# Two of six pairs of weight blocks in chunks 2 to 5 computed as seven half-size products

## The chip, the cores and the metric

One core of a Trainium2 chip. The metric is the device time of one execution in microseconds (us), as a median over executions. Most executions of a kernel agree within 0.3%; now and then one is some per cent longer, and those are left out. Profile times ("span") run from the first to the last instruction and are some 2 us shorter than the measured time. TensorE multiplies matrices, VectorE, ScalarE and GpSimd work elementwise; in profile lines they are PE, DVE, ACT and POOL, and PEld is TensorE's loading of weights.

## The reference, cut to what matters

Attention with keys and values averaged over 8 positions, then a gated feed-forward layer:

```python
q, k, v: (8 batches, 8 heads, 576, 64)
k_p, v_p = mean of 8 neighbours of k, v              # 72 keys per head
x = softmax(q @ k_p.T / 8) @ v_p                     # -> 4608 tokens x 512
h = relu(x @ w_gate) * (x @ w_val)                   # 512 -> 1536, twice
out = h @ w_out                                      # 1536 -> 512
```

## The kernel before

The 4608 tokens pass in nine chunks (0 to 8) of 512. While TensorE computes the hidden layer of chunk c, it also takes the output product of chunk c-1 and the attention of the next batch. Values are f16, sums in PSUM f32. Below, a unit is a block of the hidden layer or an output product in the order of the chunk's program; pieces of attention stand between units.

A block of the hidden layer is 128 of its 1536 columns. In chunks 0 to 5 each of twelve blocks is computed plainly:

```python
def gate_val(c, fo, t0=0, n=TCH):
    ...
    for w in (wg_sb, wv_sb):
        t = ps_mm.tile([P, TCH], F32, ...)           # one PSUM bank
        ... nc.tensor.matmul(out=t[...], lhsT=w[:, ci, fsl], rhs=x_T[...])   # 4 of 512 columns
        ps.append(t)
    nc.scalar.activation(out=relu[:, :n], in_=ps[0][:, :n], func=AF.Relu)
    nc.vector.tensor_tensor(out=h_tiles[c][:, fo, ...], in0=ps[1][:, :n], in1=relu[:, :n], op=ALU.mult)
```

The output product of every chunk already uses a scheme of the Strassen-Winograd kind: split both matrices in four, form sums of quarters, and seven half-size products do the work of eight. It needs four sums of h (`S`, two instructions each, VectorE) and four of the weights (`T`, once):

```python
sums = [... add(k, x, y, op, half)
        for k, x, y, op in ((0, d1, d, ALU.add), (1, S[0], a, ALU.subtract),
                            (2, a, d1, ALU.subtract), (3, b, S[1], ALU.subtract))
        for half in range(2)]
...
SUMS_AT = [1, 2, 3, 4, 5, 6, 13, 14]     # after which unit of the chunk each of the eight stands
```

In chunks 7 and 8, and at the end of 6, the hidden layer uses such a scheme too. Between these units stand the pieces of attention values. A piece fills two PSUM banks, and VectorE empties each with a reciprocal and a multiplication; the next piece waits for a free bank of three:

```python
def values(b, t):
    for half in range(2):
        ps = ps_at.tile([P, 512], F32, name="at_ps", tag="at_ps")     # bufs=3
        ... matmuls into ps ...
        nc.vector.reciprocal(out=rd[:n, half], in_=pv[:, :, D:D + 2])
        nc.vector.tensor_tensor(out=x[...], in0=..., in1=rd[...], op=ALU.mult)
```

GpSimd averages k and v in "trees" of additions and issues their loads.

The softmax here doesn't subtract the row's maximum and nothing guards it: scores larger than these inputs give would overflow.

## Time and profile before

| | before |
|---|---|
| time, median of 3 | 328.61 us (328.54 to 330.12) |
| span | 327.4 us, full clock |
| TensorE, VectorE, GpSimd busy | 97%, 69%, 63% |
| chain of waits: TensorE, VectorE | 89%, 6% |
| length of chunks 2, 3, 4, 5 | 34.98, 33.79, 34.00, 34.21 us |

A chunk's length is read from the timeline of TensorE, from the start of its k transposes to those of the next chunk. The lines behind the other rows, and how they are read, are in the prediction.

### The profile page before, as it was taken

How to read it: one execution, taken by the hardware profiler on the slowest of the kernel's cores; microseconds unless marked ns; L12 is line 12 of the kernel's file. 1: busy time of each engine (PE TensorE's matmuls, PEld its weight loads, DVE VectorE, ACT ScalarE, POOL GpSimd, SP SyncE). 2: the span in 40 equal slices, each digit the busy share in tenths (PEclk: the TensorE clock that was granted, in tenths of full speed). 3: DMA queues.
4: the chain of work that ended last, by engine and by line, in shares of the span. 5: the costliest groups of instructions: out<-in, count | busy, mean ns of one | idle time of the engine just before them, and what ended most of it. 6: DMA issues, size and time to landing. Idle time of an engine off the chain costs nothing.

```text
span 327.4 us, 7013 instructions
## 1 busy us (share of the span) xinstructions
PE 318.7 (97%) x2670; PEld 226.9 (69%) x2670; DVE 226.2 (69%) x482; ACT 151.2 (46%) x353; POOL 206.9 (63%) x258
## 2 busy tenths in 40 slices
PE   8899999999999999999999999999999999999995
PEld 3577885455566656665898867655667888888674
DVE  7465737677684864696387745784779989879762
ACT  1454482364466226612672257225825565565330
POOL 8556607999999942965199309999901577667300
PEclk9999999999999999999999999999999999999999
DMA  7999998996958538999794472223012130130035
GB/s 110 186 203 202 200 211 151 200 173 118 187 101 159 100 91 86 78 154 160 159 169 76 87 104 60 33 47 124 3 24 50 34 96 2 22 111 2 10 112 137
DMA packets 51010, 35.46 MB, mean 108 GB/s; under 512 B 30432, under 2 KB 45024, under 8 KB 50976
## 3 DMA queue, kind: packets, MB, share of 16 engines
q0 software_dynamic: 18304, 18.88, 36.5%
q1 hardware_dynamic: 32528, 16.00, 26.2%
q8 instruction: 21, 0.34, 0.4%
q10 hardware_dynamic: 144, 0.13, 0.1%
q14 instruction: 13, 0.11, 0.1%
HBM read 37.75 MB, written 9.44 MB: 144 GB/s over the span
## 4 chain that ended last, share of the span: by engine, by line
PE 89%; DVE 6%; DMA 2%; issue 1%; POOL 1%; ACT 0%; DVEq 0%; POOLq 0%
PE mm_ps L430 42%; PE acc_ps L523 19%; PE mm_ps L742 9%; PE at_ps L311 4%; PE mm_ps L468 3%; PE at_ps L389 3%; PE mm_ps L602 2%; DMA q<-in_q_dram 2%; PE at_ps L742 2%; DVE px L395 1%; DVE sum L514 1%; DVE h L439 1%; PE mm_ps L412 1%; PE mm_ps L366 1%; DVE px L758 1%
## 5 line engine op out<-in xcount | busy, mean ns | idle before, releaser
L439 DVE TENSOR_TENSOR h<-mm_ps,relu 128x512 f16<-128x512 f32 (+1 forms) x96 | 59.8, 624 | 69.5 <-PE mm_ps L430 59.2
L436 ACT ACTIVATE relu<-mm_ps 128x512 f16<-128x512 f32 (+1 forms) x96 | 52.2, 544 | 100.1 <-PE mm_ps L430 94.6
L430 PE MATMUL mm_ps<-x_T,wv_sb 128*128 128x512 f16 (+1 forms) x432 | 88.4, 332 | 0.4 <-DVE kpT0u L264 0.4
L430 PE MATMUL mm_ps<-x_T,wg_sb 128*128 128x512 f16 (+1 forms) x432 | 88.5, 331 | 0.0
L430 PEld LDWEIGHTS <-wv_sb 128*128 128x128 f16 x432 | 42.1, 98 | 31.2 <-DVE kpT0u L264 0.8
L430 PEld LDWEIGHTS <-wg_sb 128*128 128x128 f16 x432 | 38.9, 97 | 19.7 <-issue 0.3
L325 ACT ACTIVATE expT<-at_ps 72x288 f16<-72x288 f32 (+2 forms) x128 | 38.8, 374 | 14.3 <-PE at_ps L311 14.2
L523 PEld LDWEIGHTS <-sum 128*128 128x128 f16 x336 | 32.0, 98 | 6.3 <-DVE sum L514 0.9
L395 DVE TENSOR_TENSOR px<-at_ps,prd 128x256 f16<-128x256 f32 (+1 forms) x80 | 33.8, 423 | 2.7
L181 POOL TENSOR_TENSOR tree_b<-tree_a 72x256 f32<-72x256 f32 (+1 forms) x42 | 33.5, 797 | 3.3
L764 POOL TENSOR_TENSOR h<-px 128x256 f16<-128x256 f16 x36 | 25.4, 718 | 13.8 <-ACT px L761 12.8
L175 POOL TENSOR_TENSOR tree_a<-k_in 96x512 f32<-96x512 f16 x18 | 21.5, 1196 | 15.2 <-DMA k_in<-in_k_dram 15.2
L523 PE MATMUL acc_ps<-wo_sums,sum 128*128 128x256 f16 x252 | 30.9, 272 | 0.0
L175 POOL TENSOR_TENSOR tree_a<-v_in 72x512 f32<-72x512 f16 x24 | 28.7, 1197 | 0.1
L523 PEld LDWEIGHTS <-h 128*128 128x128 f16 x252 | 23.7, 98 | 2.9
L763 POOL TENSOR_SCALAR px<-px 128x256 f16<-128x256 f16 x12 | 13.0, 1080 | 18.1 <-PE mm_ps L742 15.3
L844 POOL COPY gate<-h 128x1 f16<-128x1 f16 x4 | 1.5, 380 | 33.9 <-DVE h L439 33.9
L523 PE MATMUL acc_ps<-wo_sb,h 128*128 128x256 f16 x168 | 20.6, 272 | 0.0
L514 DVE TENSOR_TENSOR sum<-h 128x768 f16<-128x768 f16 x28 | 19.0, 679 | 0.0
L531 DVE TENSOR_TENSOR rows<-acc_ps,mid 128x512 f32<-128x512 f32 x21 | 14.4, 686 | 4.7 <-PE acc_ps L523 4.6
L389 PEld LDWEIGHTS <-expT 72*128 72x128 f16 (+1 forms) x280 | 12.9, 100 | 5.9 <-DVE prd L394 0.8
L394 DVE RECIPROCAL prd<-at_ps 128x4 f32<-128x4 f32 (+1 forms) x80 | 13.7, 171 | 3.7 <-PE at_ps L389 3.6
(144 smaller groups left out, 527.9 us busy)
## 6 DMA issues: line engine op xcount, KB each, us to landing
out_dram<-rows SPq DMA_DIRECT2D x24, 256.0 KB
k_in<-in_k_dram POOLq DMA_DIRECT2D x7, 576.0 KB, 7.0
q<-in_q_dram POOLq DMA_DIRECT2D x7, 576.0 KB, 10.0
v_in<-in_v_dram POOLq DMA_DIRECT2D x6, 576.0 KB, 12.7
wg_sb<-in_moe_w_gate_dram POOLq DMA_DIRECT2D x6, 256.0 KB, 11.0
wv_sb<-in_moe_w_val_dram POOLq DMA_DIRECT2D x6, 256.0 KB, 10.8
wo_sb<-in_moe_w_out_dram POOLq DMA_DIRECT2D x3, 512.0 KB, 10.7
v_in<-in_v_dram POOLq DMA_DIRECT2D x2, 512.0 KB, 11.9
```

The lines of the kernel that those rows point to most:

```text
L175: eng.tensor_tensor(out=cell["a"][:n], in0=src[:, :, :4 * D], in1=src[:, :, 4 * D:], op=ALU.add)
L181: eng.tensor_tensor(out=cell["c"][:n], in0=a[:n, :, :2 * D], in1=a[:n, :, 2 * D:], op=ALU.add)
L325: nc.scalar.activation(out=out_ap, in_=in_ap, func=AF.Exp, scale=EXP_SCALE)
L389: nc.tensor.matmul(out=ps[:n, c0:c0 + D + 1], lhsT=weights(b, h, t), rhs=stats[b % 2][:SP, g, s0:s0 + D + 1], start=True, stop=True,)
L395: nc.vector.tensor_tensor(out=x[:n, half * NG // 2:(half + 1) * NG // 2, :, :], in0=pv.rearrange("p g (x c) -> p g x c", x=2)[:, :, :, :D] ...
L430: nc.tensor.matmul(out=t[:, lo:hi], lhsT=w[:, ci, fsl], rhs=x_T[:, ci, x0:x0 + hi - lo], start=(ci == 0), stop=(ci == n_co - 1),)
L436: nc.scalar.activation(out=relu[:, :n], in_=ps[0][:, :n], func=AF.Relu)
L439: nc.vector.tensor_tensor(out=h_tiles[c][:, fo, t0:t0 + n], in0=ps[1][:, :n], in1=relu[:, :n], op=ALU.mult)
L514: nc.vector.tensor_tensor(out=S[k][:, i], in0=x[:, i], in1=y[:, i], op=op)
L523: nc.tensor.matmul(out=ps[:, tb, :], lhsT=lhs[:, i, tb * P:(tb + 1) * P], rhs=rhs[:, i, :], start=(first and tb == 0 and i == 0), stop=(tb ...
L742: nc.tensor.matmul(out=ps[key][:, m], lhsT=w_of(m)[:, i], rhs=xs[:, i], start=(first and m == 0 and i == 0), stop=(m == 1 and i == N_CO - ...
L764: nc.gpsimd.tensor_tensor(out=hc[:, fo_out, cols], in0=gv[:, 0], in1=gv[:, 1], op=ALU.mult)
```

## The change

The intent: in chunks 2 to 5, replace plain blocks by seven half-size products for two of the six pairs of blocks (a block and the one 768 columns on), so that TensorE does 28 matmuls of 256 columns in place of 16 of 512 for a pair. The sums of x (VectorE, four per chunk) and of the weights (GpSimd, once, in chunk 1) get buffers of their own. The two pairs (x and y below) stand at the end of the chunk. The fourth h sum moves forward, from after units 13 and 14 to after 10 and 11. Room comes from merged pools, and one weight sum is made in place. Cut to its core:

```diff
+    def pair_products(c, fo):
+        def pr1(): product("a", plain(0, fs), e, ps_mm);       keep("a", "p1")   # ScalarE copies
+        def pr5(): product("c", summed(0), x_sums[c][0], ps_mm); keep("c", "p5")
+        def pr2(): product("b", plain(1, fs), g, ps_at, "at"); take("b", "p1")   # VectorE adds
+        def pr6(): product("a", summed(1), x_sums[c][1]);      keep("a", "u2")
+        def pr3(): product("c", summed(3), h); take("c", "u2"); finish("b", fo, lo)  # relu, GpSimd mult
+        def pr7(): product("a", summed(2), x_sums[c][2]); take("a", "p5"); finish("c", fo, hi)
+        def pr4(): product("a", plain(1, fu), x_sums[c][3]); ... finish("a", n_hf + fo, hi)
+    def pair_units(c, prods, gv):
+        x, y = [pair_products(c, fo) for fo in range(E_PAIRS)]
+        return [lambda: run([x[1], x[5], x[2], x[6], x[3]]), prods[0], x[7],
+                lambda: run([y[1], y[5]]), x[4], lambda: run([y[2], y[6], y[3]]), prods[1], y[7],
+                gv, y[4]]
...
+        EARLY_SUMS_AT = [1, 2, 3, 4, 5, 6, 10, 11]
...
+            elif c < C_HIDDEN - 1:                    # chunks 2 to 5
+                more = x_sums_of(c)
+                run(more[:2])
+                units = [std[0], prods[0], std[1], std[2], prods[1], std[3], prods[2], std[4],
+                         std[5], prods[3], std[6], prods[4]] + pair_units(c, prods[5:], std[7])
...
                 if c == 1:
-                    run(sums[i:i + 1])
+                    run(sums[i:i + 1] if i < 9 else sums[9:] if i == 13 else [])
+                    if i == 11:
+                        early_weight_sums()           # eight on GpSimd
+                elif c < C_HIDDEN - 1:
+                    if i in (7, 9):
+                        more[2 + (7, 9).index(i)]()
+                    if i in EARLY_SUMS_AT:
+                        sums[EARLY_SUMS_AT.index(i)]()
```

(The seven `pr` functions are shown on one line each; `...` marks cuts.)

More of the change, by code (lines that the diff above doesn't have):

```diff
@@ L46 @@
     NI = QT // 2
+    KG_ROWS = POOL // 2
     KP = 12
@@ L58 @@
     vin_pool = ctx.enter_context(tc.tile_pool(name="vin", bufs=2))
-    tree_pool = ctx.enter_context(tc.tile_pool(name="tree", bufs=2))
+    tree_pool = ctx.enter_context(tc.tile_pool(name="tree", bufs=1))
     q16_pool = ctx.enter_context(tc.tile_pool(name="q16", bufs=2))
@@ L66 @@
     half_pool = ctx.enter_context(tc.tile_pool(name="halfp", bufs=1))
-    relu_pool = ctx.enter_context(tc.tile_pool(name="relup", bufs=3))
-    fout_pool = ctx.enter_context(tc.tile_pool(name="foutp", bufs=2))
-    pexp_pool = ctx.enter_context(tc.tile_pool(name="pexpp", bufs=2))
+    relu_pool = ctx.enter_context(tc.tile_pool(name="relup", bufs=5))
+    row_pool = ctx.enter_context(tc.tile_pool(name="rowp", bufs=4))
+    early_pool = ctx.enter_context(tc.tile_pool(name="earlyp", bufs=1))
     piece_pool = ctx.enter_context(tc.tile_pool(name="piecep", bufs=6))
@@ L88 @@
     sel_rest = const_pool.tile([P, SP], F16, name="sel_rest")
-    kg = const_pool.tile([P, QT * 2 // POOL, 2 * D], F16, name="kg")
-    warm_sb = const_pool.tile([P, TCH], F16, name="warm_sb")
+    kg = early_pool.tile([P, 4 * TCH], F16, name="early_x")[:, :QT // KG_ROWS * 2 * D].rearrange(
+        "p (g d) -> p g d", d=2 * D)
+    warm_sb = relu_pool.tile([P, TCH], F16, name="relu")
     stats = [const_pool.tile([P, NG, 4 * D], F16, name=f"stat{i}") for i in range(2)]
@@ L359, in piece_scores @@
         cols = [(j, n * IQ, IQ)] if n < NF else [(0, NF * IQ, RI), (1, NF * IQ, RI)]
-        e = pexp_pool.tile([P, H, P], F16, name="pexp")
+        e = row_pool.tile([P, DM], F32, name="row").bitcast(F16).rearrange("p (h t) -> p h t", h=H)
         for half in range(2):
@@ L472, in part @@
             if hi == n_fo:
-                o = fout_pool.tile([P, DM], F32, name="fout")
+                o = row_pool.tile([P, DM], F32, name="row")
                 if eng is nc.vector:
@@ L486 @@
     HT, HD = TCH // 2, DM // 2
-    wo_sums = const_pool.tile([P, 4, n_hf, HD], F16, name="wo_sums")
+    wo_sums = const_pool.tile([P, 3, n_hf, HD], F16, name="wo_sums")
+    WO_T = [wo_sums[:, 0], wo_sums[:, 1], wo_sb[:, :n_hf, HD:], wo_sums[:, 2]]
     def weight_sums():
@@ L492, in weight_sums @@
         g, h = wo_sb[:, n_hf:, :HD], wo_sb[:, n_hf:, HD:]
-        t1, t2, t3, t4 = [wo_sums[:, i] for i in range(4)]
+        t1, t2, t3, t4 = WO_T
         return [lambda o=o, x=x, y=y, i=slice(i, i + 2): nc.vector.tensor_tensor(
                     out=o[:, i], in0=x[:, i], in1=y[:, i], op=ALU.subtract)
-                for o, x, y in ((t1, f, e), (t2, h, t1), (t3, h, f), (t4, g, t2))
+                for o, x, y in ((t1, f, e), (t2, h, t1), (t4, g, t2), (t3, h, f))
                 for i in range(0, n_hf, 2)]
@@ L504, in out_products @@
         b, d = hc[:, n_hf:, :HT], hc[:, n_hf:, HT:]
-        S = [sum_pool.tile([P, n_hf, HT], F16, name=f"sum{i}") for i in range(4)]
+        S = [sum_pool.tile([P, n_hf, HT], F16, name=f"sum{i}") for i in range(3)]
+        S.append(S[1])
         e, g, h = wo_sb[:, :n_hf, :HD], wo_sb[:, n_hf:, :HD], wo_sb[:, n_hf:, HD:]
-        T = [wo_sums[:, i] for i in range(4)]
+        T = WO_T
         p1, u2, u3 = [mid_pool.tile([P, 2, HD], F32, name=f"mid{i}") for i in range(3)]
@@ L585, in last_products @@
         b, d = hv[:, n_hf:, :, 0], hv[:, n_hf:, :, 1]
-        S = [sum_pool.tile([P, n_hf, HT], F16, name=f"sum{i}").rearrange(
-            "p f (z t) -> p f z t", z=2) for i in range(4)]
+        S = [sum_pool.tile([P, n_hf, HT], F16, name=f"sum{i}") for i in range(3)]
+        S.append(early_pool.tile([P, 2, 3, N_CO, E_COLS], F16, name="early_w").rearrange(
+            "p m s k f -> p (m s k f)")[:, :n_hf * HT].rearrange("p (f t) -> p f t", f=n_hf))
+        S = [t.rearrange("p f (z t) -> p f z t", z=2) for t in S]
         e, g, h = wo_sb[:, :n_hf, :HD], wo_sb[:, n_hf:, :HD], wo_sb[:, n_hf:, HD:]
-        T = [wo_sums[:, i] for i in range(4)]
+        T = WO_T
         A, Bk, C = {}, {}, {}
@@ L673, with early_weight_sums @@
     F_HALF = n_hf * P
+    E_PAIRS = 2
+    E_COLS = E_PAIRS * P
+    early_w = {}
     w_sums, x_sums, mids = {}, {}, {}
+    def early_weight_sums():
+        tl = early_pool.tile([P, 2, 3, N_CO, E_COLS], F16, name="early_w")
+        fs, fu = slice(0, E_COLS), slice(F_HALF, F_HALF + E_COLS)
+        for m, w in enumerate((wg_sb, wv_sb)):
+            s1, s2, s4 = [tl[:, m, i] for i in range(3)]
+            a11, a12 = w[:, :N_CO, fs], w[:, N_CO:, fs]
+            a21, a22 = w[:, :N_CO, fu], w[:, N_CO:, fu]
+            early_w[m] = [s1, s2, a21, s4]
+            for o, x, y, op in ((s1, a21, a22, ALU.add), (s2, s1, a11, ALU.subtract),
+                                (s4, a12, s2, ALU.subtract), (a21, a11, a21, ALU.subtract)):
+                nc.gpsimd.tensor_tensor(out=o, in0=x, in1=y, op=op)
     def hidden_weight_sums():
@@ L686, in hidden_weight_sums @@
         w_sums[0], w_sums[1] = views[:4], views[4:]
-        for f0 in range(0, F_HALF, 2 * P):
+        for f0 in range(E_COLS, F_HALF, 2 * P):
             fs, fu = slice(f0, f0 + 2 * P), slice(F_HALF + f0, F_HALF + f0 + 2 * P)
@@ L697, in x_quarters @@
     def x_quarters(c):
-        x0 = c * TCH % RING
-        return [x_T[:, k * N_CO:(k + 1) * N_CO, x0 + t * HT:x0 + (t + 1) * HT]
-                for k in range(2) for t in range(2)]
+        at = [(c * TCH + t * HT) % RING for t in range(2)]
+        return [x_T[:, k * N_CO:(k + 1) * N_CO, x0:x0 + HT] for k in range(2) for x0 in at]
     def x_sums_of(c):
         e, f, g, h = x_quarters(c)
-        x_sums[c] = [exp_pool.tile([P, 2, HS], F16, name="expT").rearrange(
-            "p x s -> p (x s)")[:, :N_CO * HT].rearrange("p (k t) -> p k t", k=N_CO)
-            for _ in range(4)]
+        if c < C_HIDDEN - 1:
+            tl = early_pool.tile([P, 4 * TCH], F16, name="early_x").rearrange(
+                "p (x k t) -> p x k t", x=4, k=N_CO)
+            x_sums[c] = [tl[:, i] for i in range(4)]
+        else:
+            x_sums[c] = [exp_pool.tile([P, 2, HS], F16, name="expT").rearrange(
+                "p x s -> p (x s)")[:, :N_CO * HT].rearrange("p (k t) -> p k t", k=N_CO)
+                for _ in range(4)]
         t1, t2, t3, t4 = x_sums[c]
@@ L717, in take_mids @@
                      :, :4 * TCH].bitcast(F32).rearrange("p (x t) -> x p t", x=2)]
-        tiles += [fout_pool.tile([P, DM], F32, name="fout") for _ in range(2)]
+        tiles += [row_pool.tile([P, DM], F32, name="row") for _ in range(2)]
         for z in range(2):
@@ L751, in summed @@
         def summed(i):
-            return lambda m: w_sums[m][i][:, :, fs]
+            return lambda m: (early_w if fo < E_PAIRS else w_sums)[m][i][:, :, fs]
         def take(key, mid, fo_out, cols, eng=None):
@@ L808, in hidden_products, with product, plain, summed @@
         return dict(enumerate((pr1, pr2, pr3, pr4, pr5, pr6, pr7, end, later), 1))
+    def pair_products(c, fo):
+        if c not in h_tiles:
+            h_tiles[c] = h_pool.tile([P, n_fo, TCH], F16, name="h")
+        hc = h_tiles[c]
+        fs, fu = slice(fo * P, (fo + 1) * P), slice(F_HALF + fo * P, F_HALF + (fo + 1) * P)
+        e, f, g, h = x_quarters(c)
+        lo, hi = slice(0, HT), slice(HT, TCH)
+        ps, mid, gv = {}, {}, {}
+        def product(key, w_of, xs, pool=None, name="mm"):
+            first = pool is not None
+            if first:
+                ps[key] = pool.tile([P, TCH], F32, name=f"{name}_ps", tag=f"{name}_ps").rearrange(
+                    "p (m t) -> p m t", m=2)
+            for m in range(2):
+                for i in range(N_CO):
+                    nc.tensor.matmul(
+                        out=ps[key][:, m], lhsT=w_of(m)[:, i], rhs=xs[:, i],
+                        start=(first and m == 0 and i == 0), stop=(m == 1 and i == N_CO - 1),
+                        skip_group_check=True,
+                    )
+        def plain(k, cols):
+            return lambda m: (wg_sb, wv_sb)[m][:, k * N_CO:(k + 1) * N_CO, cols]
+        def summed(i):
+            return lambda m: early_w[m][i][:, :, fs]
+        def keep(key, name):
+            mid[name] = row_pool.tile([P, DM], F32, name="row").rearrange("p (m t) -> p m t", m=2)
+            nc.scalar.copy(mid[name], ps[key])
+        def take(key, name):
+            gv[key] = relu_pool.tile([P, TCH], F16, name="relu").rearrange("p (m t) -> p m t", m=2)
+            nc.vector.tensor_tensor(out=gv[key], in0=ps[key], in1=mid[name], op=ALU.add)
+        def finish(key, fo_out, cols):
+            nc.scalar.activation(out=gv[key][:, 0], in_=gv[key][:, 0], func=AF.Relu)
+            nc.gpsimd.tensor_tensor(
+                out=hc[:, fo_out, cols], in0=gv[key][:, 0], in1=gv[key][:, 1], op=ALU.mult)
+        def pr1():
+            product("a", plain(0, fs), e, ps_mm)
+            keep("a", "p1")
+        def pr5():
+            product("c", summed(0), x_sums[c][0], ps_mm)
+            keep("c", "p5")
+        def pr2():
+            product("b", plain(1, fs), g, ps_at, "at")
+            take("b", "p1")
+        def pr6():
+            product("a", summed(1), x_sums[c][1])
+            keep("a", "u2")
+        def pr3():
+            product("c", summed(3), h)
+            take("c", "u2")
+            finish("b", fo, lo)
+        def pr7():
+            product("a", summed(2), x_sums[c][2])
+            take("a", "p5")
+            finish("c", fo, hi)
+        def pr4():
+            product("a", plain(1, fu), x_sums[c][3])
+            relu = relu_pool.tile([P, TCH], F16, name="relu")[:, :HT]
+            nc.scalar.activation(out=relu, in_=ps["a"][:, 0], func=AF.Relu)
+            nc.vector.tensor_tensor(
+                out=hc[:, n_hf + fo, lo], in0=ps["a"][:, 1], in1=relu, op=ALU.mult)
+            finish("a", n_hf + fo, hi)
+        return dict(zip((1, 2, 3, 4, 5, 6, 7), (pr1, pr2, pr3, pr4, pr5, pr6, pr7)))
@@ L1008 @@
                 units = weave_units(gv[:-1], o[5:])
+            elif c < C_HIDDEN - 1:
+                prods, sums = out_products(c - 1)
+                more = x_sums_of(c)
+                run(more[:2])
+                std = [gv[fo] for fo in range(n_fo) if fo % n_hf >= E_PAIRS]
+                units = [std[0], prods[0], std[1], std[2], prods[1], std[3], prods[2], std[4],
+                         std[5], prods[3], std[6], prods[4]] + pair_units(c, prods[5:], std[7])
+                gv[-1] = lambda: None
             elif c < C_HIDDEN:
@@ L1065 @@
                 if i == 3 and c + 2 < B:
-                    prep_k(c + 2, c + 3 < B, h_tiles[c][:, 1, :1] if c > 1 else None)
+                    prep_k(c + 2, c + 3 < B, h_tiles[c][:, 3, :1] if c > 1 else None)
                 if i == prep_v_at and c + 2 < B:
```

## The prediction

> **What bounds the kernel now.** I read the page first (busy shares, slices, chain), then busy time per stage, then the chain of waits in order of time, then the instructions of one chunk in order of time, and last the groups of instructions with their shapes kept apart.
>
> The page and the table by stage:
>
> ```profile
> span 327.4 us, 7013 instructions
> PE 318.7 (97%) x2670; PEld 226.9 (69%) x2670; DVE 226.2 (69%) x482; ACT 151.2 (46%) x353; POOL 206.9 (63%) x258
> ...
> PE 89%; DVE 6%; DMA 2%; issue 1%; POOL 1%; ACT 0%; DVEq 0%; POOLq 0%
> ...
> core 0: us, PE busy (x) PEld busy (x) DVE busy (x) ACT busy (x) POOL busy (x), PEclk, DMA share, GB/s
> 86.00:120.00 34.00, 33.95 (x264) 21.17 (x263) 23.99 (x53) 14.65 (x33) 30.25 (x39) 1.00 0.65 118
> 120.00:153.00 33.00, 33.00 (x249) 20.85 (x248) 22.11 (x45) 14.72 (x32) 19.63 (x25) 1.00 1.08 115
> ```
>
> TensorE holds 89% of the chain and is occupied for the whole of chunks 2 to 5 (86 to 221 us, near 34 us each; the two rows are chunks 2 and 3), at full clock. VectorE has 10 us of idle time in such a chunk. A change that removes TensorE work here should pay directly, unless another engine becomes late at some point inside a chunk. So the average of VectorE isn't enough; I looked where its idle time lies. Chunk 3, VectorE in order of time:
>
> ```profile
> 137.43 0.69 DVE L439 TENSOR_TENSOR h<-mm_ps,relu 128x512 f16<-128x512 f32 x1 [0.93 <-PE mm_ps L430]
> 139.29 0.69 DVE L439 TENSOR_TENSOR h<-mm_ps,relu 128x512 f16<-128x512 f32 x1 [1.17 <-PE mm_ps L430]
> 139.90 0.17 DVE L394 RECIPROCAL prd<-at_ps 128x4 f32<-128x4 f32 x1
> 140.11 0.42 DVE L395 TENSOR_TENSOR px<-at_ps,prd 128x256 f16<-128x256 f32 x1
> 140.45 0.17 DVE L394 RECIPROCAL prd<-at_ps 128x4 f32<-128x4 f32 x1
> 140.65 0.42 DVE L395 TENSOR_TENSOR px<-at_ps,prd 128x256 f16<-128x256 f32 x1
> 141.00 0.68 DVE L531 TENSOR_TENSOR mid<-acc_ps,mid 128x512 f32<-128x512 f32 x1
> 141.59 0.17 DVE L394 RECIPROCAL prd<-at_ps 128x4 f32<-128x4 f32 x1
> ...
> 147.71 0.42 DVE L395 TENSOR_TENSOR px<-at_ps,prd 64x256 f16<-64x256 f32 x1
> 148.57 0.69 DVE L439 TENSOR_TENSOR h<-mm_ps,relu 128x512 f16<-128x512 f32 x1 [0.44 <-PE mm_ps L430]
> 149.18 0.58 DVE L514 TENSOR_TENSOR sum<-h,sum 128x768 f16<-128x768 f16 x1
> ```
>
> In brackets is the idle time before an instruction. From 139.3 to 148.1 us VectorE has next to none: five pieces of attention values (two reciprocals and two multiplications each) pass between the h products and the additions. It keeps up with TensorE, with nothing over; its slack lies before 139 and after 148.6. The same stretch is in the other chunks. The costs, by start-to-start distances here (instructions overlap a little, so they are shorter than the printed durations): one 128x512 operation from PSUM 0.60 (139.29 to 139.90), one values piece 1.10 (139.90 to 141.00), a 128x768 sum about 0.6.
>
> **What the Trainium skill says.** "TensorE: Matmul & The Clock Gate", section "Back-to-back issue gap", gives an isolated gap of N/2.4 + 2.5 ns: 216 for 512 columns, 109 for 256, but also a sustained 131 ns for 512. The chain here agrees with the first (5.18/24 = 0.216 us; 1.31/12 = 0.109 us), not with 131:
>
> ```profile
> 119.03 5.18 PE mm_ps L430 x24
> ...
> 264.94 1.31 PE mm_ps L742 x12
> ```
>
> So halving the columns costs TensorE nothing. "VectorE: DVE Perf Modes", section "The perf-mode tier table", holds tensor_tensor from PSUM to mode 1x and lets 16-bit SBUF operands run at 2x. The trace agrees: 0.68 us for 128x512 out of PSUM, 0.42 for the same size f16 at best. "GPSIMD Engine Reference", section "Specifications", says GpSimd's SBUF interface is shared with VectorE where the latter has two SBUF inputs. The trace agrees: a 128x768 sum takes 0.55 us beside an idle GpSimd and 1.43 beside its weight sums. "Perfetto Trace Analysis", section "Identifying the Most-Contended Engine", warns that matmul busy share isn't a measure of headroom; I therefore count matmuls, not busy time.
>
> **The change part by part.** All numbers in us.
>
> 1. TensorE, removed and added. A pair of blocks is now 2 blocks x 2 matrices x 4 = 16 matmuls of 512 columns: 16 x 0.216 = 3.46. It becomes 7 products x 2 matrices x 2 = 28 of 256 columns: 28 x 0.109 = 3.05. That is 0.41 per pair and, with two pairs in four chunks, 8 x 0.41 = 3.3 in all: 1.0%. The gain can't be more than this, plus small waits that fall away (part 5).
>
> 2. VectorE, added per chunk. Each pair had two h products (2 x 0.60); it gets three additions of a PSUM bank to a kept product (the like in today's last chunks is 0.68, 0.60 apart) and one 128x256 h product (0.42). That is +1.0 a pair. Four sums of x of 128x512 f16 come on top (0.42 to 0.77 each). Together about +4 on 22 per chunk of 33, on average harmless.
>
> 3. Where these stand. In the order of the built program, one x sum and both halves of the fourth h sum now stand among the values pieces (the h sums stood after them), and the first pair's three additions come right behind or between these. From the h product at 139.29 in chunk 3's old times to the addition that frees the first pair's bank "a" for its fourth product, the VectorE queue holds: 2 h products 1.2, 5 values pieces 5.5, 3 additions of output products 1.8, 1 x sum 0.5, 2 h sums 1.2, 3 additions of the pair 1.8, sum 12.0, so it ends at about 151.3. TensorE, undisturbed, passes 144.4 where the pair starts; then five products 2.18, a values piece 0.3, an output product 1.31, the seventh product and two of the second pair 1.31: it wants to start the fourth product at 149.4. So it must lose about 1.9, wherever the wait shows. I expect parts of it at the values matmuls (at_ps has three banks, which VectorE frees in turn), the rest at the fourth product. Behind it the queue has slack again (second pair, a whole block of 1.73), so nothing more is lost. Per chunk: +1.9 - 0.82 = +1.1; and 3 x 1.1 = 3.3 for chunks 3 to 5.
>
> 4. Chunk 2 has its values pieces one unit later (pieces of the batch before come first), two of them inside the first pair. The same count, from 106.4, gives x4 at 118.0 against 115.5, +2.5 - 0.8 = +1.7. GpSimd adds a risk there: eight weight sums of 1.15 (as L695 today) go behind its tree of chunk 1, which ended at 89.7; its trees then end near 119.4 instead of 110.3, and the first product into h can come only then. VectorE's second-pair addition reuses a buffer that this product frees: up to 0.5 more.
>
> 5. Given back. Today the late h sums hold the last output product 0.3 in chunk 2 and 0.55 in chunk 5 (VectorE slowed by GpSimd's weight sums). Moved forward, and with those weight sums started later and a third fewer, both waits should go: about -0.8.
>
> 6. Off the path: ScalarE gets six copies of 0.59 and six half-size relus of 0.41 per chunk, to 19 of 33; the third product may wait 0.1 to 0.2 for the copy of the fifth. GpSimd gets six products of 0.7 per chunk, after its trees. Buffers of scores and output rows are merged into four; in chunk 0 this is neutral or a little looser. Chunks 6 to 8 are unchanged but for eight weight sums less.
>
> Sum: 3.3 + 1.7 + 0.5 x 0.5 - 0.8 + 4 x 0.1 for the copies = +4.9 if everything is as counted. Start-to-start figures that are a tenth too long would remove half of it, since the queue's excess is a difference of two sums near 10 to 12. I therefore take two thirds: +3.
>
> **The rivals.**
>
> A: TensorE's saving arrives in full, with the small waits gone: 328.6 - 3.3 - 0.8 = 324.5. For it: TensorE is the bound everywhere, VectorE's mean stays near 80%, and the order of units (a whole block placed ahead of the last product) looks made to cover the waits. Against it: the saturated 9 us before the pair.
>
> B (mine): VectorE's queue becomes the bound for some 12 us of each chunk, and takes back more than is saved: 331 to 334.
>
> C: the second pair's GpSimd products come late, so the next chunk's first output product or first h sum waits. In chunk 2 this is near; but next comes a whole block (1.73) and seven transposes, and from chunk 3 on GpSimd ends its trees before the pair. If it happened in each chunk, 2 more each: 338. I give it little.
>
> D: a new bank of PSUM at the chunk's start waits for the last fourth product. The semaphores of the built program say otherwise (the first bank waits for nothing on VectorE), so nothing.
>
> **Range and chances.** Between A (324.5) and B with its full sum (333.5) lies most of it, weighted to B: predicted 331.5, low 325.8, high 334.8. Faster by over 2% would need 6.6, twice the work removed: 0.01. Slower by over 2% needs B in full plus C in some chunks: 0.07. The rest, 0.92, within 2%.
>
> **What would show it.** Right: in chunks 3 to 5 VectorE runs without idle time from the first values piece to the pair's third addition; TensorE's gaps of about 2 in all stand at values matmuls and at the first pair's fourth product, put down to VectorE; a chunk is about 1 longer than before; the pair's 28 matmuls take 3.05 when not held. Wrong: TensorE without gaps there and chunks 0.8 shorter (then A, and my VectorE distances or order are off); or gaps at the first output product of a chunk put down to GpSimd (C); or a lower granted clock, which nothing here foresees.

## The result, and the profile after

| | before | after |
|---|---|---|
| time, median (4 runs each) | 328.88 us | 333.46 us (333.19 to 334.08) |
| ratio of fast runs | | 1.0137 (95%: 1.0115 to 1.0159) |
| span | 327.4 | 332.3 |
| chunk 2 | 34.98 | 37.45 |
| chunk 3 | 33.79 | 35.33 |
| chunk 4 | 34.00 | 35.08 |
| chunk 5 | 34.21 | 34.45 |
| from chunk 6 to the last chunk's output product | 87.98 | 88.00 |

The kernel became 1.4% slower. All runs were at full clock. A ratio here is the mean time of one kernel's fast runs over that of the other's fast runs of the same rounds, so it isn't quite the ratio of the medians beside it.

The page of the kernel after: span, busy shares, and the chain of waits by engine.

```profile
span 332.3 us, 7233 instructions
...
PE 317.4 (96%) x2734; PEld 233.6 (70%) x2734; DVE 246.0 (74%) x514; ACT 167.2 (50%) x393; POOL 225.8 (68%) x282
...
PE 76%; DVE 15%; DMA 3%; issue 3%; POOL 2%; ACT 0%; DVEq 0%; POOLq 0%
```

VectorE's busy share rose only from 69% to 74%, yet its part of the chain went from 6% to 15%. The chain's shares aren't a measure of loss: 9 points of the span are 30 us, and the kernel lost 5. They say where the last wait ends, and that moved to VectorE.

Busy time by stage after, in about the stretches of the prediction; they are chunks 2 and 3 only to within some us, as those start at 88.63 and 126.08 here and at 89.07 and 124.05 before (columns: stretch, length, then busy time of TensorE, its weight loads, VectorE, ScalarE, GpSimd, the clock, DMA share, GB/s):

```profile
86.00:120.00 34.00, 31.51 (x264) 21.43 (x263) 28.92 (x59) 16.86 (x37) 32.41 (x37) 1.00 0.61 96
120.00:154.00 34.00, 32.35 (x265) 22.53 (x263) 28.21 (x53) 17.77 (x41) 25.97 (x35) 1.00 0.91 136
```

TensorE, which was never idle here before, now stands for 2.5 and 1.7 us, while VectorE still has 5 to 6 us of idle time in the same 34. The waits of the kernel after (engine and line, what it waited for, us in total, times, longest):

```profile
PE at_ps L391 <- DVE px L397: 3.2, 7, 0.9
...
PE mm_ps L856 <- DVE relu L874: 2.6, 4, 1.2
```

Both are VectorE: the values matmuls (L391) wait for a bank that a values multiplication frees, and the first matmul of the fourth product (L856) waits for VectorE's addition. Chunk 3, TensorE in order of time, in pairs of a line and the one that came late:

```profile
144.58 0.29 PE L391 MATMUL at_ps<-stat,expT 72*128 72x65 f16 x4
145.21 0.30 PE L391 MATMUL at_ps<-stat,expT 72*128 72x65 f16 x4 [0.34 <-DVE px L397]
...
146.65 0.29 PE L391 MATMUL at_ps<-stat,expT 72*128 72x65 f16 x4
147.85 0.30 PE L391 MATMUL at_ps<-stat,expT 72*128 72x65 f16 x4 [0.90 <-DVE px L397]
...
153.00 0.60 PE L856 MATMUL mm_ps<-early_x,early_w 128*128 128x256 f16 x4
154.01 0.38 PE L856 MATMUL mm_ps<-early_x,wg_sb 128*128 128x256 f16 x2 [0.42 <-DVE relu L874]
```

The brackets add up to 1.66, but a bracket starts at the modelled end of the work before it. By starts it is more: half a values piece takes 0.13 undisturbed (0.25 for a whole one, 141.04 to 141.29) and four half-size matmuls 0.44, so the three lines came 0.50, 1.07 and 0.57 late, 2.14 together. And VectorE in the same stretch:

```profile
140.11 1.18 DVE L737 TENSOR_TENSOR early_x<-x_T 128x512 f16<-128x512 f16 x1
141.31 0.69 DVE L441 TENSOR_TENSOR h<-mm_ps,relu 128x512 f16<-128x512 f32 x1
...
143.62 0.98 DVE L737 TENSOR_TENSOR early_x<-x_T,early_x 128x512 f16<-128x512 f16 x1
...
146.21 1.02 DVE L518 TENSOR_TENSOR sum<-h,sum 128x768 f16<-128x768 f16 x1
...
148.85 0.55 DVE L518 TENSOR_TENSOR sum<-h,sum 128x768 f16<-128x768 f16 x1
...
150.41 0.68 DVE L874 TENSOR_TENSOR relu<-at_ps,row 128x512 f16<-128x512 f32 x1
151.01 0.68 DVE L874 TENSOR_TENSOR relu<-mm_ps,row 128x512 f16<-128x512 f32 x1
...
153.29 0.67 DVE L874 TENSOR_TENSOR relu<-mm_ps,row 128x512 f16<-128x512 f32 x1
155.06 0.42 DVE L911 TENSOR_TENSOR h<-mm_ps,relu 128x256 f16<-128x256 f32 x1 [1.10 <-ACT relu L910]
```

There is no idle time in brackets from 135.63 (not shown) to the pair's third addition at 153.29; the fourth product starts when that ends, at 154.01. The queue from the h product at 141.31 to its end took 12.65 us for what the prediction counted as 12.0. The excess is in two sums out of SBUF: the x sum at 143.62 took 0.9 to the next start instead of 0.5, the h sum at 146.21 took 0.95 instead of 0.6. GpSimd at that time:

```profile
139.86 1.15 POOL L177 TENSOR_TENSOR tree_a<-v_in 72x512 f32<-72x512 f16 x1
...
143.59 0.72 POOL L183 TENSOR_TENSOR tree_b<-tree_a 72x256 f32<-72x256 f32 x1
...
146.10 0.72 POOL L183 TENSOR_TENSOR tree_b<-tree_a 72x256 f32<-72x256 f32 x1
146.90 0.65 POOL L188 TENSOR_TENSOR stat<-tree_b 72x128 f16<-72x128 f32 x1
151.62 0.67 POOL L878 TENSOR_TENSOR h<-relu 128x256 f16<-128x256 f16 x1 [4.08 <-ACT relu L877]
```

Put start and length together: GpSimd's instructions end at 141.01, 144.31 and 146.82, the three slow sums at 141.29, 144.60 and 147.23. Each sum ends 0.28 or 0.29 us (512 columns) or 0.41 us (768 columns) after the GpSimd instruction beside it, however long ago it began; the sum at 148.85, with GpSimd idle, takes 0.55. The other held sums of chunks 2 to 5 of this run end in the same way, 0.28 to 0.29 or 0.41 to 0.43 after. This is what the Trainium skill, "SBUF — State Buffer", section "Who interferes with whom", says of the port pair that the two engines share, "it's an exclusive lock": the sum waits the instruction out, and the trace agrees.

Chunk 2 loses time at a second place, its start. TensorE there:

```profile
93.06 0.32 PE L391 MATMUL at_ps<-stat,expT 72*64 72x65 f16 x4 [0.43 <-DVE px L397]
...
95.58 0.32 PE L313 MATMUL at_ps<-qT,kpT1u 128*72 128x256 f16 x2 [0.25 <-DVE px L397]
96.13 0.31 PE L313 MATMUL at_ps<-qT,kpT1l 128*72 128x288 f16 x1 [0.23 <-DVE px L397]
...
118.70 0.38 PE L856 MATMUL mm_ps<-early_x,wg_sb 128*128 128x256 f16 x2 [1.23 <-DVE relu L874]
```

and VectorE just before:

```profile
85.77 2.62 DVE L497 TENSOR_TENSOR wo_sb<-wo_sb 128x512 f16<-128x512 f16 x3
...
89.35 1.67 DVE L737 TENSOR_TENSOR early_x<-x_T,early_x 128x512 f16<-128x512 f16 x1
```

Three weight sums that the change put at the end of chunk 1, then an x sum of 1.67 beside GpSimd's trees and new weight sums, leave VectorE late for the values of chunk 2. At chunk 2's start the kernel after was 0.44 ahead of the kernel before, at its second output product 0.92 behind: 1.36 lost. The other 1.11 of chunk 2's 2.47 come later, mainly at 118.70.

### The profile page after: what moved, and what is told of

The parts are those of the page before. It is cut to its first block, busy times and chain, and to the rows that moved or that the text cites. A ratio compares the mean times of both kernels' runs of the same rounds, so it can differ in the third digit from the quotient of the medians.

```text
span 332.3 us, 7233 instructions
## 1 busy us (share of the span) xinstructions
PE 317.4 (96%) x2734; PEld 233.6 (70%) x2734; DVE 246.0 (74%) x514; ACT 167.2 (50%) x393; POOL 225.8 (68%) x282
## 4 chain that ended last, share of the span: by engine, by line
PE 76%; DVE 15%; DMA 3%; issue 3%; POOL 2%; ACT 0%; DVEq 0%; POOLq 0%
PE mm_ps L432 31%; PE acc_ps L527 14%; PE mm_ps L770 8%; PE mm_ps L856 5%; PE at_ps L313 4%; DVE px L397 4%; PE mm_ps L470 3%; DMA q<-in_q_dram 3%; DVE h L441 3%; PE mm_ps L608 2%; DVE relu L874 2%; PE at_ps L391 2%; DVE sum L518 2%; PE at_ps L770 2%; DVE prd L396 1%
## 5 line engine op out<-in xcount | busy, mean ns | idle before, releaser
L441 DVE TENSOR_TENSOR h<-mm_ps,relu 128x512 f16<-128x512 f32 (+1 forms) x80 | 48.6, 609 | 49.5 <-PE mm_ps L432 43.7
L438 ACT ACTIVATE relu<-mm_ps 128x512 f16<-128x512 f32 (+1 forms) x80 | 42.6, 533 | 59.2 <-PE mm_ps L432 57.5
L432 PE MATMUL mm_ps<-x_T,wg_sb 128*128 128x512 f16 (+1 forms) x352 | 72.0, 330 | 0.0
L432 PE MATMUL mm_ps<-x_T,wv_sb 128*128 128x512 f16 (+1 forms) x352 | 72.0, 331 | 0.0
L432 PEld LDWEIGHTS <-wv_sb 128*128 128x128 f16 x352 | 34.4, 98 | 24.5 <-DVE kpT0u L266 0.2
L878 POOL TENSOR_TENSOR h<-relu 128x256 f16<-128x256 f16 x24 | 16.6, 703 | 32.5 <-ACT relu L877 32.5
L870 ACT COPY row<-mm_ps 128x512 f32<-128x512 f32 x24 | 13.3, 587 | 20.0 <-PE mm_ps L856 20.0
L527 PE MATMUL acc_ps<-wo_sb,sum 128*128 128x256 f16 x168 | 20.6, 273 | 0.1
L527 PE MATMUL acc_ps<-wo_sums,sum 128*128 128x256 f16 x168 | 20.6, 272 | 0.0
L391 PEld LDWEIGHTS <-expT 72*128 72x128 f16 (+1 forms) x280 | 13.6, 100 | 9.7 <-DVE px L397 4.3
L391 PE MATMUL at_ps<-stat,expT 72*128 72x65 f16 (+1 forms) x280 | 16.6, 195 | 3.3 <-DVE px L397 3.2
```

The lines of the kernel that those rows point to most:

```text
L391: nc.tensor.matmul(out=ps[:n, c0:c0 + D + 1], lhsT=weights(b, h, t), rhs=stats[b % 2][:SP, g, s0:s0 + D + 1], start=True, stop=True,)
L432: nc.tensor.matmul(out=t[:, lo:hi], lhsT=w[:, ci, fsl], rhs=x_T[:, ci, x0:x0 + hi - lo], start=(ci == 0), stop=(ci == n_co - 1),)
L441: nc.vector.tensor_tensor(out=h_tiles[c][:, fo, t0:t0 + n], in0=ps[1][:, :n], in1=relu[:, :n], op=ALU.mult)
L527: nc.tensor.matmul(out=ps[:, tb, :], lhsT=lhs[:, i, tb * P:(tb + 1) * P], rhs=rhs[:, i, :], start=(first and tb == 0 and i == 0), stop=(tb ...
```

## The experiments

The theory to be tested: VectorE's queue in the stretch from the values pieces to the first pair is full, and what the change put into it (fourth h sum, x sums, additions of the pair) is paid by TensorE one for one, more so where GpSimd holds a sum up. Rivals: the pair's own chain of dependent products sets the time, wherever the sums stand; or it is simply more VectorE work in a chunk, wherever it stands.

Twelve runs of eleven kernels (e11 is e7 again) were made, in three groups, each beside runs of the kernel before on the same chip. In the first group three of eight runs of the kernel before were slow (336 to 340) and are left out; its median counted with them is 329.17. In the second one was (340.89). Unless said otherwise outputs were correct.

Chunk lengths and spans of the profiled runs, for all that follows (us):

| kernel | chunk 2 | 3 | 4 | 5 | span |
|---|---|---|---|---|---|
| before | 34.98 | 33.79 | 34.00 | 34.21 | 327.4 |
| after | 37.45 | 35.33 | 35.08 | 34.45 | 332.3 |
| fourth h sum late (e1) | 36.91 | 33.93 | 33.66 | 33.53 | 328.5 |
| and x sums earlier (e2) | 37.45 | 33.67 | 33.67 | 33.26 | 328.4 |
| one x sum twice (e3) | 37.65 | 35.50 | 35.25 | 35.31 | 334.2 |
| weight sums later (e4) | 37.04 | 35.33 | 35.06 | 34.44 | 332.1 |
| block ahead of the second pair (e5) | 36.75 | 34.96 | 34.56 | 34.08 | 330.2 |
| e5 and e1 together (e6) | 36.78 | 33.67 | 33.34 | 33.47 | 326.9 |
| e6 in chunks 3 to 5 alone (e7) | 35.22 | 33.34 | 33.34 | 33.47 | 325.4 |
| an x sum twice, in the slack (e9) | 37.44 | 35.33 | 35.06 | 34.45 | 332.7 |
| weight sums at their old place (e10) | 36.64 | 35.33 | 35.06 | 34.45 | 331.8 |
| e7, last output product later (e12) | 34.63 | 33.34 | 33.34 | 33.46 | 324.9 |

Equal code gives equal chunks to 0.02 in chunks 3 to 5, with one exception: chunk 3 of e6 and of e7 is the same code behind another chunk 2, and takes 33.67 and 33.34. Chunk 1 doesn't repeat so well: 26.69 to 27.44 in runs whose chunk 1 is the same code. In the long ones (e1, e3 and e9, and also in the kernel before) TensorE waits 0.35 to 0.58 near 65 us for a copy of VectorE (`kpT0u`); the profiled run of the kernel after has no such wait.

**e1: the fourth h sum behind the first pair.** The chunk has the same work; two instructions stand later.

```diff
-        EARLY_SUMS_AT = [1, 2, 3, 4, 5, 6, 10, 11]
+        EARLY_SUMS_AT = [1, 2, 3, 4, 5, 6, 14, 15]
```

> The two halves of the fourth h sum move behind the seventh product of the first pair, nothing else. Theory (VectorE's queue from the first values piece to the first pair's third addition is longer than TensorE's work beside it): in chunks 2 to 5 the queue loses the 1.1 to 1.6 us that the two sums take in the changed kernel, so the gaps at values matmuls and at the fourth product shrink by about that in each chunk; 333.5 becomes about 329 (328 to 330.5). Rival (the seven-product pair is slow by its own chain of dependences, copies and banks): nothing moves, 333.

Measured: 330.37 us (329.54 to 333.54), ratio 1.0065 (0.9997 to 1.0134). By the medians two thirds of the loss went with the place of two VectorE instructions; by the ratio, whose interval is wide, half of it. The chunks say it more surely. Chunks 3 to 5 fell by 1.40, 1.42 and 0.92, to below the kernel before for chunks 4 and 5. The rival of a chain inside the pair can't explain it: the pair was not touched.

**e2: e1, and the last two x sums earlier.** From after units 7 and 9 to after 2 and 5.

```diff
-                    if i in (7, 9):
-                        more[2 + (7, 9).index(i)]()
+                    if i in (2, 5):
+                        more[2 + (2, 5).index(i)]()
```

> As the first, and the last two x sums of a chunk move from the start of the values stretch to before it. Theory: another 0.5 to 1 us per chunk leaves the queue, gaps in the stretch nearly vanish (under 0.5 a chunk); about 327.5 (326 to 329). Rival (dependences in the pair): 333. Second rival (VectorE has no slack earlier either, so its work is only moved): gaps come back at the third output product, about 330.

Measured: 330.12 us, ratio 1.0038 (1.0017 to 1.0059); the second rival's figure, not the theory's. Chunks 3 and 5 did fall further (0.26 and 0.27), but chunk 2 rose by 0.54. TensorE of this run shows why:

```profile
97.30 0.32 PE L313 MATMUL at_ps<-qT,kpT1u 128*72 128x256 f16 x2 [1.55 <-DVE px L397]
```

In chunk 2 the units early in the chunk aren't slack: GpSimd's weight sums run there, and the x sum moved in beside them made the values late. "Earlier" is only free where both engines have room.

**e3: one x sum twice, in the full stretch.** The fourth x sum is computed again after unit 9, into the same place.

```diff
                     if i in (7, 9):
                         more[2 + (7, 9).index(i)]()
+                    if i == 9:
+                        more[3]()
```

> The fourth x sum is made twice in chunks 2 to 5, the result stays right. Theory: VectorE's queue sets the time there, so its 0.42 to 0.98 us per chunk comes out in full: 4 x 0.65, about 336 (335 to 337). Rival (dependences in the pair, or TensorE): 333.5, as VectorE is busy only 74% of the span.

Measured: 335.86 us, ratio 1.0211 (1.0183 to 1.0239), 2.4 us above the kernel after and near what the theory said. But the chunks grew unevenly, by 0.20, 0.17, 0.17 and 0.86, 1.4 together; the rest of the difference in span (1.9) arose in chunk 1, whose code is the same. VectorE shows why the chunks grew unevenly. First chunk 5 of the kernel after, then e3, two lines of chunk 3 and two of chunk 5:

```profile
214.03 0.59 DVE L737 TENSOR_TENSOR early_x<-x_T,early_x 128x512 f16<-128x512 f16 x1
...
216.24 0.55 DVE L518 TENSOR_TENSOR sum<-h,sum 128x768 f16<-128x768 f16 x1
```

```profile
144.38 1.57 DVE L737 TENSOR_TENSOR early_x<-x_T,early_x 128x512 f16<-128x512 f16 x2
...
147.57 0.60 DVE L518 TENSOR_TENSOR sum<-h,sum 128x768 f16<-128x768 f16 x1
...
215.13 1.46 DVE L737 TENSOR_TENSOR early_x<-x_T,early_x 128x512 f16<-128x512 f16 x2
...
218.20 0.55 DVE L518 TENSOR_TENSOR sum<-h,sum 128x768 f16<-128x768 f16 x1
```

In chunk 5 the h sum was short and stayed short: the doubled x sum is 0.87 longer (1.46 for 0.59) and the chunk 0.86 longer, one for one. In chunk 3 the doubled x sum adds 0.59 to 0.98, but the h sum after it now starts only 0.2 us before the end of the GpSimd instruction that had held it (147.57 and 147.76) and takes 0.60 instead of 1.02: net 0.17, which is what the chunk grew by. So the queue is paid one for one, as it really ran, waits for GpSimd included.

**e4: the three late weight sums in chunk 2.** They go from the end of chunk 1 to after units 5 to 7 of chunk 2.

```diff
-                    run(sums[i:i + 1] if i < 9 else sums[9:] if i == 13 else [])
+                    run(sums[i:i + 1] if i < 9 else [])
...
+                        late_wo = sums[9:]
...
+                    if c == 2 and i in (5, 6, 7):
+                        late_wo[(5, 6, 7).index(i)]()
```

> The last three weight sums for the output product move from the end of chunk 1 into chunk 2, behind units 5 to 7. Theory: the 1.4 us that the changed kernel loses between the first and the second output product of chunk 2 come from these three (2.6 us together at a busy GpSimd) ahead of h products and x sums; about 1 of it returns, some comes back in the values stretch: 332.6 (331.8 to 333.2). Rival (that loss is from the first x sums alone): 333.5.

Measured: 333.46 us, ratio 1.0144 (1.0123 to 1.0166), the same as the kernel after: a miss. The gaps at 93 to 96 us went, but the fourth output product waited 0.29 for a weight sum, and the values matmuls at 111 us 0.61 instead of 0.19; chunk 2 was 0.41 shorter, where about 1 was expected. So the three sums are part of VectorE's backlog at the start of chunk 2, and most of the loss moved with them.

**e5: a whole block between the first pair's seventh product and the second pair.** The order inside the last units changes, nothing else.

```diff
-        return [lambda: run([x[1], x[5], x[2], x[6], x[3]]), prods[0], x[7],
-                lambda: run([y[1], y[5]]), x[4], lambda: run([y[2], y[6], y[3]]), prods[1], y[7],
-                gv, y[4]]
+        return [lambda: run([x[1], x[5], x[2], x[6], x[3]]), prods[0], x[7], gv,
+                lambda: run([y[1], y[5]]), x[4], lambda: run([y[6], y[2], y[3]]), y[7],
+                prods[1], y[4]]
```

> Only the order at the end of a chunk changes: the whole block stands between the seventh product of the first pair and the second pair (it stood before the second pair's last product), and the second pair's products come in the order 1, 5, 4 of the first, 6, 2, 3, 7, output product, 4. Theory: VectorE still makes TensorE wait at the values matmuls, but has 1.7 us to catch up before the fourth product; the gaps there (0.4 to 1.4 us a chunk, 3.2 in all) go: 330.5 (329.5 to 331.5). Rival (the pair's own dependences): the time stays or grows, since nothing of VectorE's work changes.

Measured: 331.91 us, ratio 1.0087 (1.0061 to 1.0112), a little above the range. In chunks 3 to 5 the gap at the fourth product is gone; the gaps at the values matmuls, which come before the moved units, stand as they were. TensorE in chunk 3 of this run, all that is left of its gaps there:

```profile
144.34 0.30 PE L391 MATMUL at_ps<-stat,expT 72*128 72x65 f16 x4 [0.33 <-DVE px L397]
...
146.97 0.30 PE L391 MATMUL at_ps<-stat,expT 72*128 72x65 f16 x4 [0.90 <-DVE px L397]
```

So the wait has two parts with two remedies: the values' part is set by what stands ahead of the values (e1), the fourth product's by how soon TensorE comes for it (e5).

**e6: both.** The edits of e1 and e5 together.

> The order of e5 and the late h sums of e1. Theory: the gaps at values matmuls go by e1, those at the fourth product by e5; what is left is the loss at the start of chunk 2: 328.5 (327.5 to 329.5), no better than the kernel before because chunk 2 still loses 1.4 at its start and 1 more to GpSimd.

Measured: 329.79 us (328.70 to 331.98), ratio 1.0042 (1.0005 to 1.0079), a little above the range. In chunks 3 to 5 no gap of TensorE stands in brackets, and they take 33.67, 33.34 and 33.47: 1.5 less than before in all. (By starts one values piece of chunk 3 still takes 0.57 for 0.25.) The time is no better than before's because of chunk 2, which is still 1.8 longer, with the gaps at its start and a wait of 1.23, now at the second pair's fourth product. One line of TensorE and two of VectorE show where this wait comes from:

```profile
122.93 0.38 PE L856 MATMUL mm_ps<-early_x,wg_sb 128*128 128x256 f16 x2 [1.23 <-DVE relu L874]
...
117.36 1.56 DVE L518 TENSOR_TENSOR sum<-h,sum 128x768 f16<-128x768 f16 x1
...
120.96 0.69 DVE L874 TENSOR_TENSOR relu<-at_ps,row 128x512 f16<-128x512 f32 x1 [0.64 <-POOL h L878]
```

VectorE's additions of the second pair came late, behind an h sum held up by a GpSimd tree (1.56 for 0.55) and by 0.64 for a GpSimd product into h, which GpSimd began only at 120.26, after its last tree. The expectation had foreseen this as "1 more to GpSimd".

**e7: the pairs in chunks 3 to 5 alone.** e6, with chunk 2 as it was before; GpSimd's weight sums go to after unit 15 of chunk 2, when its trees are done.

```diff
-            elif c < C_HIDDEN - 1:
+            elif 2 < c < C_HIDDEN - 1:
...
+                if c == 2 and i == 15:
+                    early_weight_sums()
```

> As e6, but chunk 2 stays as in the kernel before and GpSimd makes the weight sums at its end, where it was idle. Theory: chunks 3 to 5 each get the 0.8 us of TensorE that the products save, chunk 5 another 0.5 from its h sums: 3 x 0.8 + 0.5 = 2.9 less than the kernel before, ratio about 0.991 (0.989 to 0.995). If the pair cost something that I have not seen, the ratio is 1.00 or above.

Measured: 327.90 us (327.11 to 332.22, six runs, one of them slow), ratio 0.9971 (0.9934 to 1.0009), which is above the range expected; the profiled run's span is 325.4, 2.0 below before's. Chunk 2 is still 0.24 longer than before: its last output product waits 0.42 for an h sum.

**e8: e2 without GpSimd's k trees for batches 5 and on.** The output was meant to be wrong, though the record marks it as correct; there is one run. It asks whether GpSimd is what makes the sums long.

```diff
-            run(pool_k(b, i, nc.gpsimd))
+            run(pool_k(b, i, nc.gpsimd) if b < 5 else [])
```

> Wrong result on purpose: e2 without GpSimd's trees of k for the last three batches, which in e2 ran beside VectorE's h and x sums at the start of chunks 3 to 5 (t4 took 2.22 us in chunk 3, an h sum up to 1.3). Theory (GpSimd slows VectorE's sums of two SBUF operands): where GpSimd is idle these sums take 0.42 (x) and 0.55 (h). Rival (they are slow by their place in the queue or by DMA): they stay at 0.8 to 2.2. The time is not what is asked; about 328 to 330.

Measured: 329.23 us, one run. VectorE at the start of chunk 3, first of e2, then of e8:

```profile
127.53 0.90 DVE L518 TENSOR_TENSOR sum<-h 128x768 f16<-128x768 f16 x1
...
131.05 1.08 DVE L518 TENSOR_TENSOR sum<-h 128x768 f16<-128x768 f16 x1
...
136.66 2.22 DVE L737 TENSOR_TENSOR early_x<-x_T,early_x 128x512 f16<-128x512 f16 x1
```

```profile
126.97 0.54 DVE L518 TENSOR_TENSOR sum<-h 128x768 f16<-128x768 f16 x1
...
130.49 0.55 DVE L518 TENSOR_TENSOR sum<-h 128x768 f16<-128x768 f16 x1
...
136.10 1.33 DVE L737 TENSOR_TENSOR early_x<-x_T,early_x 128x512 f16<-128x512 f16 x1
```

GpSimd is idle from 126.2 to 130.3 and then copies one column and issues loads; the first two sums take 0.54 and 0.55, little more than half the time. The third didn't become short, because GpSimd's v trees came forward into the place of the k trees and were again beside it. The same sums, the same data: their length is GpSimd's doing, but the time gained is small, as VectorE has room there.

**e9: the work of e3 where VectorE has slack.** The second x sum again, after unit 1, in chunks 3 to 5.

```diff
+                    if i == 1 and c > 2:
+                        more[1]()
```

> One x sum is made twice in chunks 3 to 5, as in e3, but the second time behind the first block of the chunk, where VectorE stood idle for 1 to 1.7 us. Theory (only the stretch from the values pieces to the pair counts): 0.4 to 0.8 us more of VectorE's work per chunk and no time: 333.5 (333.0 to 334.0). Rival (any VectorE work costs): 335 to 336 as e3.

Measured: 334.57 us (333.90 to 334.67, and a slow run of 343.50 left out), ratio 1.0156 (1.0131 to 1.0181). The intervals of this and of the kernel after overlap, but the median is above what I expected. The chunk lengths settle it: 35.33, 35.06 and 34.45, as in the kernel after, with 0.77 us more of VectorE work in each. Chunk 5 is the contrast to e3: 0.86 longer there, not at all here. The gaps of chunk 3 are the old ones, to the hundredth:

```profile
148.35 0.30 PE L391 MATMUL at_ps<-stat,expT 72*128 72x65 f16 x4 [0.90 <-DVE px L397]
...
154.51 0.38 PE L856 MATMUL mm_ps<-early_x,wg_sb 128*128 128x256 f16 x2 [0.42 <-DVE relu L874]
```

The 0.5 us between the two profiled runs had arisen before chunk 2 began, in chunk 1, where both have the same code. So "more VectorE work anywhere" falls; what counts is where it stands.

**e10: the weight sums in chunk 1 at their old places, with a fourth buffer.** The room is taken from the merged row buffers.

```diff
-    row_pool = ctx.enter_context(tc.tile_pool(name="rowp", bufs=4))
+    row_pool = ctx.enter_context(tc.tile_pool(name="rowp", bufs=3))
-    wo_sums = const_pool.tile([P, 3, n_hf, HD], F16, name="wo_sums")
-    WO_T = [wo_sums[:, 0], wo_sums[:, 1], wo_sb[:, :n_hf, HD:], wo_sums[:, 2]]
+    wo_sums = const_pool.tile([P, 4, n_hf, HD], F16, name="wo_sums")
+    WO_T = [wo_sums[:, i] for i in range(4)]
-                    run(sums[i:i + 1] if i < 9 else sums[9:] if i == 13 else [])
+                    run(sums[i:i + 1])
```

> The fourth weight sum for the output product gets its own buffer again (rows from four to three buffers to make room), so its three instructions go back to their places in chunk 1 and do not wait for the end of its output rows. Theory: VectorE's backlog at the start of chunk 2 is what loses 1.4 there; e4 only moved it inside that backlog. Out of it, chunk 2's start loses under 0.3, chunk 1 gives 0.4 of it back: 332.6 (332.1 to 333.0). Rival (the loss comes from the first x sums, or from the rows' buffers): 333.5 or more.

Measured: 333.46 us (332.44 to 333.72), ratio 1.0123 (1.0100 to 1.0146): mostly a miss. The gaps at the start of chunk 2 are gone and the chunk is 0.81 shorter, so the in-place sums did cost something there; a values gap of 0.67 later in the chunk took some back, and chunk 1 began 0.45 later. Whether that is the third row buffer missing in chunk 0 or chance stays open.

**e11: e7 again, five rounds.** Its ratio in e7 was too wide.

> The kernel of e7 once more, to narrow its interval: ratio 0.994 to 0.997 if the profile's 2.0 us less than before are what the runs show in the same state.

Measured: 327.74 us, ratio 0.9951 (0.9931 to 0.9971), in the range. Faster than before by half a per cent. Its profiled run was a slow one and isn't read.

**e12: e7, and the last output product of chunk 2 one block later.** This goes after the wait of 0.42 that e7 left.

```diff
-                    if prods and fo not in (1, 4, 7, 10):
+                    if prods and fo not in ((1, 4, 7, 9) if c == 2 else (1, 4, 7, 10)):
```

> e7 with the last output product of chunk 2 one block later, since it waited 0.4 to 0.6 us for VectorE's second half sum: 0.4 less than e11, ratio 0.993 to 0.996.

Measured: 326.70 us (326.36 to 327.15, six runs), ratio 0.9924 (0.9905 to 0.9943), a little better than expected. This beats both kernels: by the medians 2.4 us under before and 6.8 under after. Its page, and its busy time in chunk 3:

```profile
span 324.9 us, 7164 instructions
...
PE 88%; DVE 4%; ACT 2%; issue 2%; DMA 2%; POOL 1%; DVEq 0%; POOLq 0%
```

```profile
120.00:154.00 34.00, 33.95 (x276) 23.39 (x274) 27.87 (x53) 18.37 (x41) 21.70 (x29) 1.00 0.98 130
```

Against the kernel after, VectorE does nearly the same in these 34 us (27.87 and 28.21), and TensorE is busy for 33.95 instead of 32.35. The chain is back on TensorE. The move of the output product wasn't run in the kernel before by itself, so a third of a microsecond of the gain (chunk 2: 34.98 to 34.63) may belong to that kernel as well.

## Why the prediction was right or wrong

The time predicted was 331.5, with 325.8 to 334.8 as the range; 333.46 lies in it, in the class with 0.92. The direction and the cause were right. By its parts:

1. *TensorE's saving, 0.41 a pair.* Right. Undisturbed, four half-size matmuls take 0.44 (147.98 to 148.42 in chunk 3 of the kernel after), so a pair's 28 take 3.06. With the gaps gone (e12) chunks 3 to 5 are 0.45, 0.66 and 0.75 shorter than before, against 0.82 counted, and 0.44 of chunk 5's 0.75 is the wait of part 5. So some 1.4 of the 2.5 counted arrived; of the rest, some 0.2 a chunk is the second pair's seventh product (in e12 0.65 after the product before it, for 0.44), by the order of the code a wait for ScalarE's copy; that wasn't tested.

2 and 3. *VectorE's queue, 1.9 lost in each of chunks 3 to 5.* Right in place and near in size. (The sum for TensorE gives 149.5, not 149.4, so 1.8.) TensorE came 2.14 late in chunk 3, at values matmuls and the fourth product as said; e12, without those gaps, is 1.99 shorter there. The net per chunk was predicted as +1.1 and came out as +1.54 and +1.08 in chunks 3 and 4; in chunk 5, where 0.55 was to be given back, +0.24 instead of +0.55. e1 and e3 show the mechanism from both sides, e9 that the same work in the slack costs nothing.

4. *Chunk 2, +1.7.* The part behind the first pair came out as 1.11. What the step lacked was the start of the chunk: 1.36 lost there to VectorE's backlog beside a busy GpSimd, so 2.47 in all. The late GpSimd product was there as foreseen: VectorE's addition at 121.26 waited 0.49 for it, without a wait of TensorE behind it.

5. *Given back, 0.8.* Right. By starts, the last output product of the kernel before took 1.53 us and came 0.16 late in chunk 2 (117.34 to 118.87), and took 1.75 in chunk 5 (219.12 to 220.87), for 1.31: 0.38 and 0.44. In the kernel after it takes 1.31 in both.

6. *ScalarE's copies, 0.1 each.* The third product didn't wait (149.29 to 149.74, four matmuls, 0.45). The term was 0.4 too large.

The step that failed is the last one: "Start-to-start figures that are a tenth too long would remove half of it ... I therefore take two thirds: +3." The full sum, +4.9, was the measured difference of the spans (+4.9; +4.6 by the medians). The figures weren't too long but too short, 12.65 for 12.0, and the reason was in the prediction's own text, a 128x768 sum of 1.43 beside GpSimd. The queue was priced with quiet sums at a time when GpSimd was running its v trees. Nor does the discount come out of the prediction's own numbers: a tenth of 12.0 is 1.2 a chunk, which in four chunks is nearly all of the +4.9, not half. That the total fits to the tenth is partly luck: the missed start of chunk 2 (+1.36) stands against the terms of chunk 2's rest (-0.6), the copies (-0.4) and a chunk 1 that was 0.53 shorter, which is within its scatter.

Of the rivals, A (324.5, the saving arrives in full) fell for this order of units; e12 shows that more than half of the saving of chunks 3 to 5 can be had by order alone. C appears in the kernel after only as the 0.49 in chunk 2; once the gap at the first pair was gone (e6), it was what made TensorE wait there. D doesn't occur: no bank at a chunk's start waits for the fourth product.

What stays open is how the loss in chunk 2 divides. e2, e4 and e10 each took one piece of work away from its start or moved one in, and the backlog shifted with it. That it goes when the pairs are left out there (e7, e12) is shown; which of the sums at its start is to blame isn't.

## What to carry to other kernels

Before work is moved to an engine with idle time, find where in the stage that idle time lies: in chunk 5 one repeated sum cost its full 0.87 us in the full stretch and nothing eight units earlier, while VectorE's busy share of the span was 74% and 75%. When such a change comes out slower, try the order first: the same instructions in another order turned 1.4% slower into 0.4% slower (e6), and leaving out the one chunk without room into 0.5% faster (e11). And give a product that needs a bank to be emptied some independent TensorE work ahead of it.

## What the Trainium skill lacked or had wrong

- "GPSIMD Engine Reference", section "Specifications", names the contention of VectorE and GpSimd without a size, and no page says how long after GpSimd's instruction a held sum of VectorE ends. Here a 128x512 f16 sum took 0.41 to 0.42 us where it wasn't held and up to 2.22 where it was, a 128x768 sum 0.54 to 0.55 and up to 2.28; a held sum ended 0.27 to 0.29 (512 columns) or 0.41 to 0.43 us (768) after GpSimd's instruction.
- "SBUF — State Buffer", section "SBUF: two separate sides", gives the pair to whichever instruction starts first. In e2 the x sum at 136.66 began while GpSimd was issuing a load, and yet ended 0.29 us after a tree instruction that began at 137.43 and took 1.16. Why it lost its turn isn't shown.
- "TensorE: Matmul & The Clock Gate", section "Back-to-back issue gap": its sustained 131 ns for 512 columns was not seen; streams ran at 216 ns, its isolated figure.
- No page gives the size by which the idle time printed before a matmul falls short of the delay: three gaps of 1.66 us in brackets were 2.14 by starts.
